# High parts of the weight pieces one step ahead of the low parts, and a down ring turned by two banks

## The chip, the cores and the metric

The kernel runs on one core of a Trainium2 chip. The metric is the device time of one execution in microseconds (us). Three timed runs of the kernel before gave 2814.41 us as their median, with 2812.03 and 2814.73 us as the lowest and the highest. One more execution was recorded by the profiler; its own time was 2820.96 us and its span, from the first to the last recorded instruction, 2819.2 us.

## The reference

The program is one pre-norm transformer block in float32 on 2048 rows of width 576: softmax attention with 32 heads of 18 columns, then a gated feed-forward layer with 4608 hidden columns.

```python
h  = x + attention(layernorm(x), wqkv, wo)            # 32 heads, full softmax
n  = layernorm(h)                                     # no scale, no offset
g, u = n @ w_gate, n @ w_up                           # 576 -> 4608, both
h2 = h + (gelu(g) * u) @ w_down                       # 4608 -> 576
```

Only the feed-forward layer is touched by the change. It fills about the last 1200 us of the span.

## The kernel before, in words

**Numbers in two parts.** TensorE multiplies float16. To keep float32 precision every operand is scaled by a power of two and split: a high part (the value rounded to float16) and a low part (what the rounding left). A product is then the sum of high by high, low by high and high by low. For weights, ScalarE (ACT) writes the high part with one activation, and VectorE (DVE) writes the low part with one `scalar_tensor_tensor`, which reads the weight and the high part. The power of two comes from the largest magnitude of the piece: two DVE reductions, a transpose on TensorE (PE), and six to fifteen tiny DVE operations ("the tail").

**Chunks and units.** The 4608 hidden columns are cut into 18 chunks of 256, and two chunks make a pair. The rows are taken in two halves (0 and 1). `unit(c, p)` computes gate and up products of chunk c for one half, by a Strassen scheme: seven block products for gate, seven for up, each of seven 512-column matmuls. It has 14 steps, called m1 to m14 here, and each ends with a `yield`. It uses six PSUM banks: `g[0..2]` = `singles[0..2]` and `u[0..2]` = `more[0..2]`. After the products, ACT applies gelu, DVE multiplies by the up product ("gate", line 907), ACT writes the high part of the result (line 910) and POOL the low part (line 913). The last of these in a unit belong to `ag` and `au`: the DVE adds of lines 965 and 970, the gelu of line 904, the gate of line 907.

`down(p, dsc, last)` then multiplies the results of two chunks by two chunks of `w_down`: 16 products of twelve 288-column matmuls, each product into the next bank of `down_ring`, and each followed by one DVE operation (line 989) that adds it to the rows in `nat` and so frees the bank. A bank is taken again after four products. The twelve matmuls of one product take, for f = 0 to 3 in turn, (high result, `dh[f]`), (high result, `dl[f]`), (low result, `dh[f]`); `dh` and `dl` are the high and low part of `w_down`.

**The order of the work.** PE, ACT, DVE, POOL and the queue of SP run the instructions in the order in which the program emits them (`manual_schedule`). The preparation of the next weights is a chain of generators called `side`; `beside(main, side)` emits one step of the main generator and then one step of `side`. So a side step decides behind which main instructions its own instructions stand on each engine.

- `split_matrix(c, m)` prepares gate (m = 0) or up (m = 1) of chunk c: five steps of `exponents` (a reduction in the first; a reduction in the second; the transpose in the fifth), a "ready" step with the tail, and three steps that each write the high and low part of some of the seven pieces (lines 826 to 837). In the first of these (k = 0) `then()` starts the load of the next matrix into the same buffer `W8`; for the last matrix it stands at k = 2 and loads `w_down` (line 854).
- `split_down` prepares `w_down`: five steps of `exponents`, one with the tail (lines 862 to 872), four that write `dh[f]` and `dl[f]`, and at the end `blank_rows()`, a small memset on POOL.

One pair runs as `unit(c, 1)` beside the first six steps of the next gate matrix; then `unit(c+1, 1)`, `down(1)`, `unit(c+2, 0)` and `unit(c+3, 0)` beside one chain (line 1117); then `down(0)` beside nothing. The chain has 13 slots in `unit(c+1, 1)` (none after m14), 14 in `down(1)` (none after its first two products), and 14 in each of the two units: 55. It needs

```python
g2 3, pause 2, u2 9, pause 2, g3 9, pause 2, u3 9, pause 5, dn 10     # sum 51
```

slots, where g2, u2 are gate and up of chunk c+2, g3, u3 of chunk c+3, and dn is `split_down`. What is left of the chain when the last unit ends is emitted at once (`run(dn)`), ahead of `down(0)`. The same generators, with the same pauses of five, prepare the first chunks in a longer chain (line 1079) that ends with `rows1()`, which makes the rows of half 1.

Of the kernel before, what the change touches and what calls it, by code (L numbers as in the profile page):

```python
# [14 lines left out]
AF = mybir.ActivationFunctionType  # L15
# [16 lines left out]
def tile_block(  # L32
# [18 lines left out]
    nc = tc.nc  # L51
# [22 lines left out]
    singles = [ps.tile([P, 512], F32, name=f"bank{i}") for i in range(4)]  # L74
# [4 lines left out]
    def ring(items):  # L79
        while True:  # L80
            yield from items
# [12 lines left out]
    def view(region, off, shape, dtype=None):  # L94

        dtype = dtype or region.dtype
        v = region if dtype == region.dtype else region.bitcast(dtype)
        size = 4 if dtype == F32 else 2
        n = math.prod(shape)
        assert off % size == 0  # L100
        v = v[:, off // size : off // size + n]
        if len(shape) == 2:
            v = v.rearrange("p (a b) -> p a b", b=shape[1])
        elif len(shape) == 3:
            v = v.rearrange("p (a b c) -> p a b c", b=shape[1], c=shape[2])
        return v
# [11 lines left out]
    def exponents(views, name, space=2):  # L118

        after = 1 if space == 2 else 0  # L120
        n = len(views)
        k = views[0].shape[1]
        ac = small.tile([P, n, k], F32, tag=f"ac{n}_{k}", name=f"ac_{name}")
        am = small.tile([P, n], F32, tag=f"am{n}", name=f"am_{name}")
        for i, v in enumerate(views):
            for c in range(k):
                nc.vector.tensor_reduce(ac[:, i, c : c + 1], v[:, c], axis=AX.X, op=ALU.max,
                                        apply_absolute_value=True)
                if i + 1 < n or c + 1 < k:
                    yield  # L130
        nc.vector.tensor_reduce(am, ac, axis=AX.X, op=ALU.max)
        for _ in range(2 * space - after):
            yield
        pt = next(m_ring)
        for i in range(n):
            nc.tensor.transpose(pt[:, i * P : (i + 1) * P], am[:, i : i + 1].to_broadcast([P, P]), id32)
        for _ in range(after):
            yield
        ab = small.tile([P, n], F32, tag=f"ab{n}", name=f"ab_{name}")
        nc.vector.tensor_reduce(ab, pt[:, : n * P].rearrange("o (n p) -> o n p", n=n),  # L140
                                axis=AX.X, op=ALU.max)
        nc.vector.tensor_scalar_max(ab, ab, 2.0 ** -60)
        e = small.tile([P, n], I32, tag=f"e_{name}", name=f"e_{name}")
        nc.vector.tensor_scalar(e, ab.bitcast(I32), 23, None, op0=ALU.logical_shift_right)
        return e
# [139 lines left out]
    def result(it):  # L285
        while True:
            try:
                next(it)
            except StopIteration as end:
                return end.value  # L290
# [114 lines left out]
    with tc.manual_schedule(engines={EngineType.SP}):  # L405
        n0, n1, n2 = norm_w(0), norm_w(1), norm_w(2)
        s = [None, None]
# [27 lines left out]
        s = [None, result(n1)]  # L435
# [335 lines left out]
    df = view(A, W8O, (4, D))  # L771
# [7 lines left out]
    dh = view(W, 6 * 2 * S, (4, D), F16)  # L779
    dl = view(W, 6 * 2 * S + 2 * 4 * D, (4, D), F16)  # L780
# [3 lines left out]
    def blank_rows():  # L784
        nc.gpsimd.memset(W8[3 * KR :, 4:, 2], 0.0)
# [14 lines left out]
    def split_matrix(c, m, hi_on=None, then=None, at=0, space=2):  # L800

        wh, wl = slots[c % 2][m]
        sums = [(nc.gpsimd.tensor_add, S1, A21, A22), (nc.gpsimd.tensor_sub, S2, S1, A11),
                (nc.gpsimd.tensor_sub, S3, A11, A21), (nc.gpsimd.tensor_sub, S4, A12, S2)]

        def add():
            if sums:
                op, d, a, b = sums.pop(0)
                op(W8[:, d], W8[:, a], W8[:, b])  # L809

        it = exponents([view(A, W8O + 4 * 4 * KT * P, (2, 2 * KT * P))], f"m{m}", space)
        while True:
            add()
            try:
                next(it)
            except StopIteration as end:
                e = end.value
                break
            yield
        while sums:  # L820
            add()
        nc.vector.tensor_copy(ee[:, m, c % 2 : c % 2 + 1], e)
        s = pow2(e, -1, 266, f"s_m{m}")
        yield "ready"
        r = slice(2 * KR, 3 * KR)
        for k, (a, b) in enumerate(((4, 7), (0, 2), (2, 4))):
            if hi_on is None:
                nc.scalar.activation(wh[:, a:b], W8[:, a:b], AF.Copy, scale=s)  # L828
            else:
                hi_on(wh[:, a:b], W8[:, a:b], s)  # L830
            nc.vector.scalar_tensor_tensor(wl[:, a:b], W8[:, a:b, :2], s, wh[:, a:b, :2],  # L831
                                           op0=ALU.mult, op1=ALU.subtract)
            nc.vector.scalar_tensor_tensor(wh[r, a:b, 2], W8[r, a:b, 2], s[r], wh[r, a:b, 2],  # L833
                                           op0=ALU.mult, op1=ALU.subtract)
            if k == at and then is not None:
                then()
            yield
        if m == 0:
            scales[c % 2] = (pow2(e, 1, -20, f"gsc{c % 2}"), pow2(e, -1, 228, f"hsc{c % 2}"))
# [9 lines left out]
    def pause(n):  # L849
        for _ in range(n):  # L850
            yield
# [7 lines left out]
    def split_down(sc):  # L859

        ed = yield from exponents([view(A, W8O + 4 * 2 * D * i, (1, 2 * D)) for i in range(2)], "dn")
        E = small.tile([P, 2], I32, tag="E", name="E")
        nc.vector.tensor_add(E, ee[:, 0], ee[:, 1])
        nc.vector.tensor_add(ed, ed, E)
        M = small.tile([P, 1], I32, tag="M", name="M")
        nc.vector.tensor_max(M, ed[:, 0:1], ed[:, 1:2])
        nc.vector.tensor_sub(E, E, M.to_broadcast([P, 2]))
        nc.vector.tensor_scalar(E, E, 1, 268, op0=ALU.mult, op1=ALU.add)
        nc.vector.tensor_scalar_max(E, E, 0)
        s = pow2(E, 1, 0, "s_dn")  # L870
        dscs.append(pow2(M, 1, -262, "dsc"))
        yield
        for f in range(4):
            sf = s[:, f // 2 : f // 2 + 1]
            nc.scalar.activation(dh[:, f], df[:, f], AF.Copy, scale=sf)
            nc.vector.scalar_tensor_tensor(dl[:, f], df[:, f], sf, dh[:, f],
                                           op0=ALU.mult, op1=ALU.subtract)
            yield
        blank_rows()
# [133 lines left out]
    side = iter(())  # L1013
# [6 lines left out]
    for n in range(NS):  # L1020
# [3 lines left out]
        for kt in range(NT):  # L1024
# [28 lines left out]
            if n == 2 and kt == 4:  # L1053
                side = prepare_wo()
# [3 lines left out]
            if n == NS - 2 and kt == NT // 2:  # L1058
                by = nc.vector.tensor_scalar_mul
                side = chain(split_matrix(0, 0, by, lambda: load_matrix(w_up, 0, nc.gpsimd), space=6), pause(10),  # L1060
                             split_matrix(0, 1, by, lambda: load_matrix(w_gate, 1, nc.gpsimd), space=6),
                             pause(10), until_ready(second))
# [11 lines left out]
    more = [ps2.tile([P, 512], F32, name=f"more{i}") for i in range(4)]  # L1074
    banks += singles[:3] + more[:3]
    m_ring = ring([singles[3], more[3]])
    down_ring = ring([singles[1], more[1], singles[0], more[0]])
    it = unit(0, 0)
    side = chain(second, pause(5), split_matrix(1, 1, None, lambda: load_down(0, nc.gpsimd), 2),
                 pause(5), split_down(0), rows1())  # L1080
# [22 lines left out]
    for sc in range(NCH // 2):  # L1103
        c = 2 * sc
        last = sc == NCH // 2 - 1
        dsc = dscs[-1]
        if not last:
            g2, g3 = (split_matrix(c + 2, 0, None, lambda c=c: load_matrix(w_up, c + 2)),
                      split_matrix(c + 3, 0, None, lambda c=c: load_matrix(w_up, c + 3)))
            u2, u3 = (split_matrix(c + 2, 1, None, lambda c=c: load_matrix(w_gate, c + 3)),  # L1110
                      split_matrix(c + 3, 1, None, lambda sc=sc: load_down(sc + 1), 2))
            dn = split_down(sc + 1)
            side = chain(until_ready(g2))
        beside(unit(c, 1), side)
        run(side)
        if not last:
            side = chain(g2, pause(2), u2, pause(2), g3, pause(2), u3, pause(5), dn)
        beside(islice(u := unit(c + 1, 1), 13), side)
        run(u)
        beside(down(1, dsc, last), side, head=2)  # L1120
        if last:
            break
        run(u2)
        beside(unit(c + 2, 0), side)
        run(u3)
        beside(unit(c + 3, 0), side)
        run(dn)
        if sc + 2 < NCH // 2:
            load_matrix(w_gate, c + 4)
        beside(down(0, dscs[-1], sc == NCH // 2 - 2), iter(()))  # L1130
# [26 lines left out]
```

## Time and profile before

| what | value |
|---|---|
| median of three runs | 2814.41 us (2812.03 to 2814.73) |
| profiled execution: time, span | 2820.96 us, 2819.2 us |
| granted TensorE clock, mean over the span | 0.987 |
| PE busy, share of the span | 94% |
| DVE, ACT, POOL busy | 78%, 54%, 24% |
| PE busy in 200 us of the feed-forward part | 196.5 to 196.9 us |
| distance of one pair from the next | 134.8 us |

A row of the timeline gives the start and length of an instruction (or of a run of equal ones), its engine, its line, what it writes and reads, and in brackets the idle time of the engine before it with the engine, tile and line that ended the wait. A row of the waits gives the total, the number and the longest. "PEclk" is the TensorE clock granted, as a share of full speed. [...]

### The profile page before, as it was taken

Reading aid. Unit: us, or ns where it says so; the run is one execution under the profiler, and the core shown is the slowest. Engines: PE = TensorE matmul, PEld = TensorE weight load, DVE = VectorE, ACT = ScalarE, POOL = GpSimd, SP = SyncE. Lnnn points to the kernel's source line nnn. Section 1 sums busy time; section 2 is a strip of 40 time slices with the busy share of each in tenths; the row PEclk is TensorE's granted clock in tenths of the full one; section 3 lists DMA queues with packets and bytes.
Section 4 is the critical chain, followed back from the end, with each engine's and each line's share of the span. In section 5 each row is a group of like instructions: output and inputs, shape, how many; then the busy total and the mean of one; then the engine's idle time right before and its main releaser. Section 6 shows DMA issues by size and latency. Waiting matters only on the chain.

```text
span 2819.2 us, 43701 instructions
## 1 busy us (share of the span) xinstructions
PE 2645.4 (94%) x16665; PEld 1094.8 (39%) x16665; DVE 2188.8 (78%) x3950; ACT 1515.8 (54%) x1872; POOL 682.9 (24%) x833
## 2 busy tenths in 40 slices
PE   6899999999999999999997789999999999999999
PEld 3542222222222222222233345555555555555555
DVE  6369999999999999999978657575757575656563
ACT  5216877777777777777754324333334333333332
POOL 2101432211222122211215333232322222322211
PEclk9999999999999999999999899999999999999999
DMA  8211110100101010000014131010101010101011
GB/s 220 75 50 41 39 39 14 29 19 15 39 12 36 14 39 14 25 22 18 25 30 110 53 76 48 11 48 21 39 21 40 22 46 21 38 22 38 21 57 39
DMA packets 162823, 111.99 MB, mean 40 GB/s; under 512 B 82612, under 2 KB 141620, under 8 KB 162612
## 3 DMA queue, kind: packets, MB, share of 16 engines
q1 hardware_dynamic: 150479, 95.30, 12.3%
q0 software_dynamic: 7296, 12.66, 1.7%
q8 instruction: 130, 2.13, 0.3%
q10 hardware_dynamic: 4837, 1.25, 0.2%
q14 instruction: 81, 0.66, 0.1%
HBM read 74.45 MB, written 14.42 MB: 32 GB/s over the span
## 4 chain that ended last, share of the span: by engine, by line
DVE 51%; PE 42%; DMA 3%; ACT 2%; issue 1%; SPq 1%; POOL 0%; ACTq 0%; DVEq 0%; POOLq 0%
DVE mx L535 42%; PE bank L899 12%; PE more L899 12%; PE bank L279 8%; PE more L279 5%; PE pair L279 4%; DVE W L833 1%; ACT W L828 1%; DMA X<-A 1%; PE bank L532 1%; DVE W L831 1%; DVE nat L989 1%; PE bank L585 1%; DVE st L186 1%; DVE WK L831 1%
## 5 line engine op out<-in xcount | busy, mean ns | idle before, releaser
L535 DVE TENSOR_REDUCE mx<-bank 128x1 f32<-128x512 f32 x2048 | 1264.9, 682 | 29.1 <-PE bank L532 29.1
L581 ACT ACTIVATE WK<-pair 128x1024 f32<-128x1024 f32 x1024 | 991.5, 1021 | 303.4 <-PE pair L579 303.1
L585 PE MATMUL bank<-WK,V 128*32 128x512 f32 x4096 | 548.3, 607 | 0.2 <-ACT nat L599 0.2
L279 PEld LDWEIGHTS <-WK 128*128 128x128 f16 x3456 | 338.7, 98 | 109.0 <-issue 16.3
L899 PEld LDWEIGHTS <-W 128*128 128x128 f16 x2394 | 235.0, 98 | 283.5 <-issue 8.2
L532 PE MATMUL bank<-W 54*128 54x512 f16 x1024 | 291.5, 382 | 40.0 <-DVE mx L535 10.0
L532 PE MATMUL bank<-A 54*128 54x512 f16 x1024 | 280.4, 382 | 37.2 <-DVE mx L535 6.3
L585 PEld LDWEIGHTS bank<-WK,V 128*32 128x32 f32 x4096 | 81.0, 108 | 437.9 <-issue 411.4
L279 PE MATMUL bank<-W,WK 128*128 128x288 f16 x1728 | 236.7, 287 | 14.2 <-DVE nat L989 10.8
L279 PE MATMUL more<-W,WK 128*128 128x288 f16 x1728 | 235.5, 286 | 3.4 <-DVE nat L989 3.4
L608 POOL TENSOR_TENSOR rp<-rc,minus_one 128x16 f32<-128x16 f32 x28 | 81.8, 2923 | 612.3 <-DMA rc<-nat 612.3
L899 PE MATMUL more<-X,W 128*128 128x512 f16 x792 | 223.8, 379 | 0.0
L899 PE MATMUL more<-V,W 128*128 128x512 f16 x720 | 203.2, 380 | 0.0
L809 POOL TENSOR_TENSOR A<-A 128x384 f32<-128x384 f32 x144 | 143.3, 1016 | 172.2 <-ACT V L920 100.4
L913 POOL TENSOR_TENSOR WK<-tmp,WK 128x512 f16<-128x512 f32 x73 | 88.0, 1206 | 332.3 <-ACT WK L910 325.2
L579 PE MATMUL pair<-W 56*128 56x512 f16 x1024 | 157.2, 379 | 3.6 <-ACT WK L581 2.8
L532 PEld LDWEIGHTS <-W 54*128 54x128 f16 x1024 | 59.7, 93 | 247.9 <-issue 219.6
L579 PE MATMUL pair<-A 56*128 56x512 f16 x1024 | 154.2, 376 | 0.2
L917 ACT COPY tmp<-bank 128x512 f32<-128x512 f32 x36 | 20.9, 582 | 237.5 <-PE bank L899 237.5
L532 PEld LDWEIGHTS <-A 54*128 54x128 f16 x1024 | 57.2, 93 | 235.1 <-issue 205.9
L828 ACT ACTIVATE W<-A,p_s_m 128x768 f16<-128x768 f32 (+1 forms) x78 | 78.2, 1036 | 105.6 <-DVE p_s_m L171 105.6
L989 DVE SCALAR_TENSOR_TENSOR nat<-more,p_dsc,nat 128x288 f32<-128x288 f32 x144 | 74.2, 515 | 77.7 <-PE more L279 77.1
(261 smaller groups left out, 2892.6 us busy)
## 6 DMA issues: line engine op xcount, KB each, us to landing
A<-in_B_w_down_dram SPq DMA_DIRECT2D x8, 1152.0 KB
nat<-rc SPq DMA_DIRECT2D x32, 256.0 KB
A<-in_B_w_gate_dram SPq DMA_DIRECT2D x64, 128.0 KB
A<-in_B_w_up_dram SPq DMA_DIRECT2D x64, 128.0 KB
qk_hi<-qk SPq DMA_DIRECT2D x36, 128.0 KB
qk_lo<-qk SPq DMA_DIRECT2D x36, 128.0 KB
out_dram<-nat SPq DMA_DIRECT2D x16, 288.0 KB
X<-nat SPq DMA_DIRECT2D x100, 36.0 KB
```

The source lines that it names most:

```text
L279: nc.tensor.matmul(dst, a, b, start=(i == 0), stop=(i == len(pairs) - 1))
L532: nc.tensor.matmul(pms[j][:, :TB], Q[r, q0 : q0 + P], K[r, kc * TB : (kc + 1) * TB], start=True, stop=True)
L535: nc.vector.tensor_reduce(mx[:, t, 2 * pr + j, kc : kc + 1], pms[j][:, :TB], axis=AX.X, op=ALU.max)
L579: nc.tensor.matmul(pS[:, j, :TB], K[r, kt * P : (kt + 1) * P], Q[r, qc * TB : (qc + 1) * TB], start=True, stop=True)
L581: nc.scalar.activation(pes[(2 * kt + pr) % NPE], pS[:, :, :TB], AF.Exp, scale=ex_reg)
L585: nc.tensor.matmul(acc[32 * hh : 32 * hh + 32, :TB], Vg[n // NB][:, kt * G4 + hh * VC : kt * G4 + hh * VC + 32], pes[(2 * kt + hh // 2) % ...
L608: nc.gpsimd.tensor_tensor(rc, den, minus_one.to_broadcast([P, R]), op=ALU.pow)
L809: op(W8[:, d], W8[:, a], W8[:, b])
L828: nc.scalar.activation(wh[:, a:b], W8[:, a:b], AF.Copy, scale=s)
L899: nc.tensor.matmul(bank, w, x_, start=start and i == 0, stop=i == len(mm) - 1, skip_group_check=not start)
L913: nc.gpsimd.tensor_sub(hl[:, 2 * i + j], v, hh[:, 2 * i + j])
L989: nc.vector.scalar_tensor_tensor(nat[:, t, ws], pt[:, :HALF], dsc, nat[:, t, ws], op0=ALU.mult, op1=ALU.add)
```

## The change

For weights whose high part ACT writes, the high part of the first piece is now emitted in a step of its own, and each later step emits the high part of the next piece together with the low part of the present one. So `split_matrix` has four such steps where it had three, and `split_down` five where it had four. `then()` stays behind the low part of its k, one step later than before. Weights whose high part DVE itself writes (the first two matrices, `hi_on` given) keep their order.

`down_ring` starts with `singles[0], more[0]` in place of `singles[1], more[1]`, so that of the 16 products the last two go to `singles[1]` and `more[1]` rather than to `singles[0]` and `more[0]`. The pause ahead of dn is four steps where it was five (line 1117 only). The chain of a pair now needs

```python
g2 4, pause 2, u2 10, pause 2, g3 10, pause 2, u3 10, pause 4, dn 11  # sum 55
```

```diff
@@ split_matrix
-        for k, (a, b) in enumerate(((4, 7), (0, 2), (2, 4))):
+
+        def high(a, b):
             if hi_on is None:
                 nc.scalar.activation(wh[:, a:b], W8[:, a:b], AF.Copy, scale=s)
             else:
                 hi_on(wh[:, a:b], W8[:, a:b], s)
+
+        cuts = ((4, 7), (0, 2), (2, 4))
+        if hi_on is None:
+            high(*cuts[0])
+            yield
+        for k, (a, b) in enumerate(cuts):
+            if hi_on is not None:
+                high(a, b)
+            elif k + 1 < len(cuts):
+                high(*cuts[k + 1])
             nc.vector.scalar_tensor_tensor(wl[:, a:b], W8[:, a:b, :2], s, wh[:, a:b, :2],
                                            op0=ALU.mult, op1=ALU.subtract)
@@ split_down
         yield
+        sf = [s[:, f // 2 : f // 2 + 1] for f in range(4)]
+        nc.scalar.activation(dh[:, 0], df[:, 0], AF.Copy, scale=sf[0])
+        yield
         for f in range(4):
-            sf = s[:, f // 2 : f // 2 + 1]
-            nc.scalar.activation(dh[:, f], df[:, f], AF.Copy, scale=sf)
-            nc.vector.scalar_tensor_tensor(dl[:, f], df[:, f], sf, dh[:, f],
+            if f < 3:
+                nc.scalar.activation(dh[:, f + 1], df[:, f + 1], AF.Copy, scale=sf[f + 1])
+            nc.vector.scalar_tensor_tensor(dl[:, f], df[:, f], sf[f], dh[:, f],
                                            op0=ALU.mult, op1=ALU.subtract)
             yield
         blank_rows()
@@ the rings and the chain
-    down_ring = ring([singles[1], more[1], singles[0], more[0]])
+    down_ring = ring([singles[0], more[0], singles[1], more[1]])
-            side = chain(g2, pause(2), u2, pause(2), g3, pause(2), u3, pause(5), dn)
+            side = chain(g2, pause(2), u2, pause(2), g3, pause(2), u3, pause(4), dn)
```

## Prediction

> **What bounds the kernel now.** The first line of the page gives the span; a windows answer over one pair then gives busy time by stage (columns: stretch, its length, then busy us and count of PE, PEld, DVE, ACT and POOL, PEclk, DMA).
>
> ```profile
> span 2819.2 us, 43701 instructions
> 2008.53:2051.15 42.62, 42.62 (x199) 19.58 (x199) 29.93 (x58) 21.86 (x34) 12.41 (x12) 1.00 0.13 41
> 2051.15:2074.67 23.52, 23.52 (x193) 18.79 (x192) 9.13 (x17) 0.76 (x2) 5.08 (x6) 1.00 0.07 21
> 2074.67:2117.20 42.53, 42.53 (x201) 19.48 (x199) 24.17 (x47) 19.56 (x30) 11.21 (x11) 1.00 0.06 18
> 2117.20:2143.43 26.23, 23.95 (x195) 18.91 (x194) 20.02 (x40) 5.91 (x7) 6.32 (x6) 1.00 0.16 46
> ```
>
> The stages are two units of half 0, `down(0)`, two units of half 1, `down(1)`. PE sets the pace and has no gap in the first three; only `down(1)` loses time, 26.23 - 23.95 = 2.28 us in a pair of 134.9. More than about 8 x 2.3 = 18 us isn't there to be won in the repeated part. The waits from 1500 us on (total, number, longest) name them.
>
> ```profile
> PE bank L279 <- DVE nat L989: 10.8, 9, 2.6
> PE bank L899 <- DVE pi_gsc L169: 9.6, 8, 1.2
> ```
>
> The timelines around the first show a relay between ACT and DVE:
>
> ```profile
> 2116.30 1.02 DVE L831 SCALAR_TENSOR_TENSOR WK<-A,p_s_m,W 128x768 f16<-128x768 f32 x1 [0.65 <-ACT W L828]
> 2117.35 1.39 DVE L833 SCALAR_TENSOR_TENSOR W<-A,p_s_m,W 32x384 f16<-32x384 f32 x1
> 2118.77 0.69 DVE L965 TENSOR_TENSOR WK<-bank,WK 128x512 f32<-128x512 f32 x1
> 2119.50 0.72 ACT L904 ACTIVATE WK<-WK,p_gsc 128x512 f32<-128x512 f32 x1 [2.72 <-DVE WK L965]
> 2120.13 0.92 ACT L828 ACTIVATE W<-A,p_s_m 128x768 f16<-128x768 f32 x1
> 2121.08 0.75 DVE L831 SCALAR_TENSOR_TENSOR WK<-A,p_s_m,W 128x512 f16<-128x512 f32 x1 [1.62 <-ACT W L828]
> 2123.75 0.51 DVE L989 SCALAR_TENSOR_TENSOR nat<-bank,p_dsc,nat 128x288 f32<-128x288 f32 x1
> 2124.31 1.63 PE L279 MATMUL bank<-W,WK 128*128 128x288 f16 x12 [1.07 <-DVE nat L989]
> ```
>
> The low part of u2 (k = 0) holds up the add at 2118.77; the gelu waits for that add, the next high part stands behind the gelu, the next low part behind that. The first down product began at 2117.20, yet its rows are added at 2123.75, and the fifth product waits for that bank.
>
> **Step 1, the ring.** At the end of `down(1)`, the 13th and the 15th product are added here:
>
> ```profile
> 2139.45 0.52 DVE L989 SCALAR_TENSOR_TENSOR nat<-bank,p_dsc,nat 128x288 f32<-128x288 f32 x1
> 2142.85 0.52 DVE L989 SCALAR_TENSOR_TENSOR nat<-bank,p_dsc,nat 128x288 f32<-128x288 f32 x1
> 2143.43 0.81 PE L899 MATMUL bank<-X,A 128*128 128x512 f16 x3 [1.20 <-DVE pi_gsc L169]
> ```
>
> The next unit starts in `singles[0]`. That is the bank of product 15 now (free at 2143.37, PE at 2143.43) and of product 13 in the changed order (free at 2139.97, before PE gets there). The scale the wait is put down to isn't read by a matmul; it only stands behind that add. Products 15 and 16 go to `g[1]`, `u[1]`, which m3 and m4 need 3 us later. At the other end `down` begins in `g[0]`, `u[0]`, last read by the gelu of m11 and the gate of m12, both over by then. So the ring takes the whole 9.6 us.
>
> **Step 2, the first wait.** u2 now has its high part in slot 13 (after m13) and its low parts in slots 14 to 16, behind down products 3 to 5. DVE goes from m12's gate to the tail, the add of m13, the add and gate of m14, and is ready for the first row add when product 1 is; the three low parts (1.02 + 0.61, then twice 0.75 + 0.48) lie between row adds of 0.51 that come every 1.47 us, and each bank is free over 2 us before it is taken again. Of the 10.8 us one 2.6 belongs to the first pair; 8.2 us go.
>
> **Step 3, what is late next.** The four matrices take four steps more, the pause gives one back: dn starts in slot 45 where it started in 42, its tail moves from 47 to 50, its last low part from 51 to 55, which is behind m14 of the last unit, directly ahead of `down(0)`. Until now 8 us of matmuls covered it. DVE rows of that unit before (tail from L140 to L171):
>
> ```profile
> 2029.78 1.67 PE L899 MATMUL bank<-X,W 128*128 128x512 f16 x7
> 2037.76 0.42 DVE L140 TENSOR_REDUCE ab_dn<-bank 128x2 f32<-128x256 f32 x1
> 2038.77 1.16 POOL L913 TENSOR_TENSOR WK<-tmp,WK 128x512 f16<-128x512 f32 x1 [5.36 <-ACT WK L910]
> 2038.88 1.07 DVE L866 TENSOR_TENSOR M<-e_dn 128x1 int32<-128x1 int32 x1
> 2041.04 0.15 DVE L171 TENSOR_SCALAR p_dsc<-pi_dsc 128x1 int32<-128x1 int32 x1
> 2044.42 0.69 DVE L946 TENSOR_TENSOR A<-bank,A 128x512 f32<-128x512 f32 x1 [1.08 <-ACT A L945]
> 2045.09 0.82 DVE L876 SCALAR_TENSOR_TENSOR W<-A,p_s_dn,W 128x576 f16<-128x576 f32 x1
> 2046.72 0.75 DVE L907 SCALAR_TENSOR_TENSOR A<-tmp,p_hsc,A 128x512 f32<-128x512 f32 x1
> 2051.15 1.63 PE L279 MATMUL bank<-W,WK 128*128 128x288 f16 x12
> ```
>
> The tail lasted 3.43 us, 0.9 of them L866 until POOL's row ended, so 2.5 alone. It now stands behind m9's add (2044.42, fixed by PE and ACT) and everything after it queues on DVE in this order: add 0.69, tail 2.5, add 0.69, gate 0.75, low 0.82, gate 0.75, low 0.82, add 0.69, low 0.82, add 0.69, gate 0.75, low 0.82: 10.8 us. From one start to the next the rows lose or gain under 0.1 us (2044.42 to 2045.09 is 0.67), so I leave the sum: the last `dl` is ready at 2055.2. No high part is later: the last follows the gelu (0.72) on the third add. The first down product reaches the matmul that reads `dl[3]`, its eleventh, at 2051.15 + 10 x 0.1225 (1.47 a product) = 2052.4. PE stands 2.8 us, and all of `down(0)` behind that matmul; DVE's row adds wait with it and lose nothing more. With 0.08 us saved at each of the eleven seams it is 2.0. POOL's three subtractions of 1.16 now run beside low parts and the last gate, as it ran beside L833 at 2117.35 (1.39 where its equal at other places takes 0.61). That row lost 0.78; 1.2 us in all is my upper bound for it, so 4.0. I take 3.2 us, nearer the plain sum: eight pairs, +25.6 us (+16 to +32).
>
> [...]
>
> **Step 4, loads and queues.** SP's load of `w_down` sits behind the low parts of u3, in slot 40 instead of 36 (6.0 us later), on a DVE about 1 us behind:
>
> ```profile
> 2025.18 0.37 SPq L854 DMA_DIRECT2D A<-in_B_w_down_dram  x1
> A<-in_B_w_down_dram POOLq DMA_DIRECT2D x1, 1152.0 KB, 6.1
> ```
>
> 2032.2 + 6.1 = 2038.3; two reductions (2.7) and 0.2 end at 2041.2, the transpose is due after m8, at 2041.9: hidden by 0.7 us, and each further us would stop PE. SP has nothing behind it until the next gate load, which waits for the last low part (2055.2 for 2048.2) and has all of `down(0)`. `blank_rows` on POOL moves behind m14, where nothing waits for it. The gate and up loads move by one to three steps and keep 2 us or more ahead of their transposes: nothing.
>
> **Step 5, the first chunks.** Their chain gets three steps more and no pause back, and low parts now fall behind the row statistics:
>
> ```profile
> 1593.49 0.79 POOL L854 DMA_DIRECT2D A<-in_B_w_down_dram  x1 [23.13 <-DVE st L186]
> 1603.11 0.43 PE L136 MATMUL more<-id,am_dn 128*128 128x128 f32 x2 [1.13 <-DVE am_dn L131]
> 1676.04 0.32 PE L136 MATMUL bank<-id,am_m 128*128 128x128 f32 x1 [2.90 <-DVE am_m L131]
> ```
>
> That load starts some 5 us later, its transpose two unit steps (3 us) later, so PE waits about 2 us more there; the rows of half 1 start later, but a copy that stood behind their transposes goes ahead. Between -2 and +5 us; I take +1.5.
>
> **Sum.** -9.6 - 8.2 + 25.6 + 1.5 = +9.3 us, on the profiled 2820.96: 2830.3. The median is 6.55 below the profiled run: 2823.7 us, say 2824.
>
> **Rivals.** *The cover is enough (other side).* If dn's tail ran two unit steps (3.0 us) earlier, in the DVE idle time before 2044.42, `dl[3]` would land in time and the gains stay: 2814.4 - 17.8 + 1.5 = 2798. It decides from a wait of 0.7 us down; for it speaks DVE's 12.7 us of idle in 42.6; against it that program order keeps the tail behind m9's add. *A wash.* At a wait of 2.2 us loss and gain cancel: 2815. For it: 2.0 is within the bounds. *The clock drops too.* After a longer stop PE ran slow:
>
> ```profile
> 1656.00:1665.00 9.00, 5.62 (x45) 4.36 (x45) 5.84 (x16) 1.00 (x2) 0.00 (x0) 1.00 0.50 97
> 1672.00:1676.00 4.00, 1.13 (x6) 0.29 (x3) 2.08 (x4) 0.00 (x0) 1.05 (x2) 1.00 0.19 54
> 1676.00:1680.00 4.00, 3.96 (x13) 1.66 (x14) 3.13 (x9) 2.30 (x4) 4.00 (x4) 0.66 0.00 0
> ```
>
> A stop of 2.90 us (row 1676.04) was followed by a granted clock of 0.66 over 4 us, 1.4 us lost; stops summing to 3.4 us in nine were not. Eight such: +11, 2835. For it: 3.2 is longer than 2.90; against: a few matmuls fall into the stop. [...] *The ring doesn't help:* if the 1.2 us is some other wait, 2833; the row adds speak against it.
>
> **How the numbers follow.** Under 0.2%, 5.6 us, a change can't be told from none. Chances: forecast (2818 to 2831) 0.50, wash 0.22, clock 0.11, cover 0.13, ring 0.04. Slower 0.62 (some of the forecast's lower edge is within 0.2%), same 0.25, faster 0.13. The likeliest case alone is 2816 to 2831; the range, with the lowest sum of the bounds (2820.96 - 17.8 + 16 - 2 less 6.55, 2811) and most of the clock's, is 2808 to 2836.
>
> **What would show it.** Right: no wait for `pi_gsc` at a unit's first product, none at the fifth of `down(1)`, DVE's waits for line 828 nearly gone, a new wait of about 3 us in each `down(0)`'s first product for `dl`'s line, pairs near 135.8 us. A `down(0)` that starts without a wait makes the prediction wrong; a wait at the transpose of dn would show Step 4 wrong.

## The result and the profile after

The changed kernel takes 2841.85 us (median of four runs, 2837.11 to 2844.21) beside 2814.47 us for the kernel before: a ratio of 1.0097 with a 95% interval of 1.0080 to 1.0115. It is slower by some 27 us; 9.3 us had been forecast, and the time lies above the stated range. In a later comparison on one chip the ratio was 1.0081 (1.0067 to 1.0095). The median of the kernel before differed from one comparison to the next (2814.5, 2819.7, 2819.7, 2821.9 us), so below each kernel is held against the kernel before that ran beside it.

The profiled executions took 2820.96 us before and 2844.21 us after: 23.25 us more. First the page's span, then the stages of one pair of chunks in the order of before: two units of half 0, `down(0)`, two units of half 1, `down(1)` (columns as before).

```profile
span 2842.4 us, 43702 instructions
2014.72:2057.34 42.62, 42.62 (x202) 19.50 (x199) 29.31 (x61) 20.00 (x33) 11.48 (x10) 1.00 0.14 45
2057.34:2085.29 27.95, 25.06 (x190) 19.21 (x189) 12.04 (x21) 2.35 (x4) 6.73 (x7) 0.94 0.09 27
2085.29:2127.83 42.54, 42.54 (x202) 19.58 (x201) 23.74 (x47) 18.53 (x29) 11.98 (x11) 1.00 0.06 18
2127.83:2151.35 23.52, 23.52 (x192) 18.68 (x191) 15.78 (x34) 6.26 (x8) 5.38 (x6) 1.00 0.11 32
```

`down(1)` has lost its gaps. `down(0)`, which had none, has taken 27.95 us in this row where it took 23.52, and its PE is idle for 2.89 us. Its clock column reads 0.94, and in spite of the idle time its busy time has grown too, from 23.52 to 25.06. The waits of PE from 1500 us on name the new one; the two rows of before (`nat L989` at the fifth product, `pi_gsc`) have no successor in the repeated part, from 1750 us on:

```profile
PE bank L279 <- DVE W L890: 23.1, 16, 1.7
```

Line 890 writes `dl`. Sixteen waits are two in each of eight pairs. Here is one on PE:

```profile
2057.34 1.02 PE L279 MATMUL bank<-W,WK 128*128 128x288 f16 x7
2059.59 0.53 PE L279 MATMUL bank<-W,WK 128*128 128x288 f16 x3 [1.23 <-DVE W L890]
2061.78 0.41 PE L279 MATMUL bank<-W,WK 128*128 128x288 f16 x2 [1.66 <-DVE W L890]
2062.02 2.71 PE L279 MATMUL more<-W,WK 128*128 128x288 f16 x12
2064.52 2.27 PE L279 MATMUL bank<-W,WK 128*128 128x288 f16 x12
```

The first product stops at its eighth matmul for `dl[2]` and at its eleventh for `dl[3]`; the two stops together are called the stop below. Then the second product takes 2064.52 - 2062.02 = 2.50 us from start to start, where one at a clock of 1.00 takes 1.47 (and is recorded with 1.63, so that neighbours overlap): the clock has dropped. Six microseconds from the end of each of the eight stops on, three of the eight rows (the eight read 0.77, 0.51, 0.72, 0.72, 0.77, 0.51, 0.72, 0.72 for PEclk):

```profile
1786.57:1792.57 6.00, 6.00 (x39) 4.33 (x39) 1.55 (x3) 0.00 (x0) 1.61 (x2) 0.77 0.38 110
1923.41:1929.41 6.00, 6.00 (x26) 3.72 (x26) 1.03 (x2) 0.00 (x0) 1.62 (x2) 0.51 0.39 113
2061.78:2067.78 6.00, 6.00 (x36) 4.25 (x36) 1.55 (x3) 0.00 (x0) 1.61 (x2) 0.72 0.40 115
```

What the clock lacks of 1.00 in the eight rows adds up to 2.56, times 6 us: 15.4 us. PE is busy for all of the 6.00 us in each of these rows; its matmuls don't wait, they only run slowly; in steps of 0.2 us the clock column reads 0.50 for 3.4 or 6.8 us at each stop and 1.00 around that.

The change did what it was made for: from 1750 us on, VectorE's waits for the high parts that ACT writes in `split_matrix` sum to 53.8 us before (line 828) and to 16.3 after (the same line is 829 there); the seven waits that are left were there before. These waits were not what set the time.

### The profile page after: what moved, and what is told of

It reads as the page before. It is cut to its first block, busy times and chain, and to the rows that moved or that the text cites. A ratio compares the mean times of both kernels' runs of the same rounds, so it can differ in the third digit from the quotient of the medians.

```text
span 2842.4 us, 43702 instructions
## 1 busy us (share of the span) xinstructions
PE 2666.9 (94%) x16665; PEld 1102.3 (39%) x16665; DVE 2170.4 (76%) x3950; ACT 1512.9 (53%) x1872; POOL 686.7 (24%) x833
## 5 line engine op out<-in xcount | busy, mean ns | idle before, releaser
L279 PEld LDWEIGHTS <-WK 128*128 128x128 f16 x3456 | 345.4, 100 | 138.9 <-issue 27.7
L279 PE MATMUL bank<-W,WK 128*128 128x288 f16 x1728 | 246.2, 292 | 31.6 <-DVE W L890 23.1
L279 PE MATMUL more<-W,WK 128*128 128x288 f16 x1728 | 245.8, 294 | 4.1 <-DVE nat L1003 4.0
L1003 DVE SCALAR_TENSOR_TENSOR nat<-bank,p_dsc,nat 128x288 f32<-128x288 f32 x144 | 74.4, 517 | 98.0 <-PE bank L279 97.1
```

The costliest lines, as they stand in the source:

```text
L279: nc.tensor.matmul(dst, a, b, start=(i == 0), stop=(i == len(pairs) - 1))
L1003: nc.vector.scalar_tensor_tensor(nat[:, t, ws], pt[:, :HALF], dsc, nat[:, t, ws], op0=ALU.mult, op1=ALU.add)
```

## The experiments

Two questions were open: what each part of the change is worth, and whether the time beyond the stop is the clock. Where a line number differs from the kernel before, the statement is the same and its line has moved.

### The ring alone (e1)

```diff
 # the kernel before
-    down_ring = ring([singles[1], more[1], singles[0], more[0]])
+    down_ring = ring([singles[0], more[0], singles[1], more[1]])
```

> The kernel before with only the ring turned. Theory (the 1.2 us at the start of a pair is a wait for the bank of the 15th down product): it goes in all eight pairs, 2814.5 - 9.6 = 2805 us, and the fifth product of down(1) still waits 1.07 us. Rival (the wait is for something else): 2814.5 us, the 1.2 us stay.

Measured: 2809.08 us beside 2819.70, ratio 0.9961 (0.9950 to 0.9972): 10.6 us less. The waits of PE from 1500 us on keep the one at the fifth product and have no row for `pi_gsc` any more:

```profile
PE bank L279 <- DVE nat L989: 10.8, 9, 2.5
```

So the wait that the profile put down to the scale was one for the 15th product's bank, as the prediction had it.

### The order alone (e2)

```diff
 # the changed kernel
-    down_ring = ring([singles[0], more[0], singles[1], more[1]])
+    down_ring = ring([singles[1], more[1], singles[0], more[0]])
```

> The changed kernel with the ring as before. Prediction as made (each part is worth its own term): the 1.2 us come back, 2841.9 + 9.6 = 2851 us. Rival (the new order alone puts the 15th product's row add ahead of the low parts of g3, so the bank is free in time without the ring): 2842 us within 3, no wait at the start of a pair.

Measured: 2843.38 us, ratio 1.0086 (1.0068 to 1.0104), with no wait at the start of a pair; the changed kernel's later ratio is 1.0081. The rival expectation held. DVE and PE at the end of a `down(1)`:

```profile
2147.52 0.52 DVE L1003 SCALAR_TENSOR_TENSOR nat<-bank,p_dsc,nat 128x288 f32<-128x288 f32 x1 [0.95 <-PE bank L279]
2147.95 1.01 DVE L842 SCALAR_TENSOR_TENSOR W<-A,p_s_m,W 128x768 f16<-128x768 f32 x1
...
2148.79 1.67 PE L913 MATMUL bank<-X,A 128*128 128x512 f16 x7
```

The 15th product's row add (2147.52) now stands ahead of g3's first low part (2147.95), so its bank is free before the next unit begins at 2148.79. The ring and the new order remove the same wait; beside the new order the ring adds nothing.

This run holds one more answer. It has the stop of the changed kernel, 2.18 or 2.19 us from one restart of PE to the next in each of the eight pairs. Seven times the six microseconds behind it read 0.50 to 0.77 for PEclk. The first time they do not:

```profile
1784.93:1790.93 6.00, 6.00 (x49) 4.79 (x49) 2.07 (x4) 0.00 (x0) 1.63 (x2) 1.00 0.37 109
```

The stop is there and the clock holds; what that pair took stands in the table of the pairs below.

### PE kept busy during the stop (e4)

Twelve matmuls into a bank that nobody reads fill the two stops; the stop itself can't shrink.

```diff
 # the changed kernel, first product of each down(0)
-                    run(accumulate(pt[:, :HALF], pairs))
+                        for q, (a, b) in enumerate(pairs):
+                            for _ in range({7: 5, 10: 7}.get(q, 0)):
+                                nc.tensor.matmul(singles[3][:, :512], id16, XT[:, 0, :512], start=True, stop=True)
+                            nc.tensor.matmul(pt[:, :HALF], a, b, start=q == 0, stop=q == 11)
```

> The changed kernel with twelve more matmuls of 512 columns, into a bank that nobody reads, in the two stops of each first product of down(0): five ahead of its 8th matmul, seven ahead of its 11th. They add 2.6 us of PE work to 2.9 us of stop, so the stop itself stays. Clock theory (the stop is followed by some 3.4 us or more at half clock, 2.0 us lost in a pair): granted clock near 1.0 after the stop, 8 x 2.0 = 16 us less, 2826 us. Rival (the time beyond the stop comes from elsewhere): 2842 us or a little more.

Measured: 2828.61 us, ratio 1.0029 (1.0017 to 1.0042), 14.8 us below e2, which has the same stops and ran beside it. The stop and the six microseconds after it:

```profile
2052.97:2057.41 4.44, 4.14 (x23) 2.15 (x22) 4.29 (x6) 2.36 (x4) 1.21 (x2) 1.00 0.01 4
2057.41:2063.41 6.00, 6.00 (x49) 4.79 (x49) 2.07 (x4) 0.00 (x0) 1.63 (x2) 1.00 0.38 106
```

The first down product still takes its 4.4 us, but the granted clock is 1.00 throughout, here and in the six microseconds behind each of the other seven stops. The time beyond the stop is the clock's.

### Cover on PE's side (e5)

```diff
 # the changed kernel, down(0)
+        if spread:
+            open_ = [(i, n, next(down_ring)) for i in range(2) for n in range(2)]
+            for i, n, pt in open_:
+                for q, (a, b) in enumerate(down_pairs(0, i, n)[:6]):
+                    nc.tensor.matmul(pt[:, :HALF], a, b, start=q == 0, stop=False)
+            for i, n, pt in open_:
+                for q, (a, b) in enumerate(down_pairs(0, i, n)[6:]):
+                    nc.tensor.matmul(pt[:, :HALF], a, b, start=False, stop=q == 5)
...
```

> The changed kernel, but the first four products of down(0) take their matmuls for f = 0 and 1 in four banks first (2.9 us of work) and those for f = 2 and 3 after that, so that the late low part has cover on PE. Theory: the stop of 2.9 us and the half clock behind it both go, 2841.9 - 23 - 16 = 2803 us. Rival (the wait only moves to a later product, or the half clock has another cause): 2825 to 2842 us.

Measured: 2811.24 us, ratio 0.9968 (0.9956 to 0.9979), 8.5 us below the kernel before. In the repeated part one short wait is left in each pair:

```profile
PE bank L1006 <- DVE W L890: 6.8, 8, 0.8
```

With 2.9 us of matmuls put in front, 23.1 us of recorded waits become 6.8, and the clock reads 1.00 behind all eight of them. The forecast of 2803 us was too low by this rest.

### dn three steps earlier, and the first chain as before (e3, e6, e8)

```diff
 # e3, and e8
-            side = chain(g2, pause(2), u2, pause(2), g3, pause(2), u3, pause(4), dn)
+            side = chain(g2, pause(1), u2, pause(1), g3, pause(1), u3, pause(4), dn)
 # e6, and e8: the first chain with high and low part in one step
-        if hi_on is None:
+        if hi_on is None and ahead:
             high(*cuts[0])
             yield
...
+    # second, split_matrix(1, 1, ...) and split_down(0) are called with ahead=False
```

> The changed kernel with the three pauses of two steps between the matrices cut to one, so that dn and all its parts come three steps (4.5 us of matmuls) earlier and the loads come earlier with them. Theory: the last low part lands in time, no stop in down(0), no half clock there: the changed kernel's time less 23 - 16, that is 15 to 18 us below the kernel before, plus 1 to 5 us for the first chain. Rival (the low parts of u2 fall back between the unit's last adds and the first wait of down(1) returns): 8 us more than that.

> The changed kernel, but the chain of the first chunks (up of chunk 1 and the first w_down, and gate of chunk 1) keeps high and low part in one step as before. Theory (the first chain got three steps longer, its w_down load and its rows of half 1 start later): 2 to 5 us less than the changed kernel. Rival (other waits of that stretch hide it): within 1 us of the changed kernel.

> Both: pauses of one between the matrices, and the first chain as before. Theory: all gains of the change and none of its costs, 15 to 18 us below the kernel before. Rival: a wait at a transpose or in down(1) takes back 8 us or more.

Measured, beside 2819.70 us: e3 2803.73 (0.9938, 0.9922 to 0.9955), e6 2840.15 (1.0066, 1.0049 to 1.0083), e8 2801.90 (0.9931, 0.9915 to 0.9948). With dn back under its cover neither e3 nor e8 has a wait in the repeated part but a single one of 1.0 us. What the first chain costs was measured once more, with the changed kernel beside it:

> The changed kernel itself, beside its variants on one chip: 1.0097 of the kernel before within 0.002, as in its first runs.

> The changed kernel with the first chain as before, beside the changed kernel: 2 to 5 us less if the longer first chain costs what Step 5 said at its upper half; under 1 us less if other waits hide it.

> The changed kernel with pauses of one between the matrices and the first chain as before, beside the others: 17 to 18 us below the kernel before.

Beside 2821.92 us: the changed kernel 2843.51 (1.0081, as expected), the same with the old first chain 2840.20 (1.0074, 1.0061 to 1.0088), with both edits 2802.59 (0.9928, 0.9914 to 0.9941). The first chain's share is 3.3 us by these medians and 1.8 by e3 and e8. The intervals of the ratios overlap in both comparisons, so it isn't shown that the longer first chain costs anything; if it does, it is a few microseconds.

### Only the pause cut (e9)

```diff
 # the changed kernel
-... u3, pause(4), dn)
+... u3, pause(1), dn)
```

> The changed kernel with the pause ahead of dn cut from four steps to one: dn comes three steps earlier, but the load of w_down does not. Theory (the load is issued 2.4 us into the last unit, takes 6.1 us, and two reductions follow, so the transpose after m5 isn't fed before 11.4 us while PE is there at 7.6): the stop in down(0) goes, and PE waits 3 to 4 us at dn's transpose instead, in all eight pairs, with a half clock after it as well: within 10 us of the changed kernel. Rival (the load has room): the same time as with the pauses of one.

Measured: 2843.86 us, ratio 1.0079 (1.0063 to 1.0096). The stop in `down(0)` is gone; PE waits for dn's reductions instead. Waits of PE from 1750 us on, then one of them and the 6 us after it:

```profile
PE bank L136 <- DVE am_dn L131: 12.3, 4, 3.3
PE more L136 <- DVE am_dn L131: 11.4, 4, 3.0
```

```profile
2044.65:2047.68 3.03, 0.00 (x1) 0.00 (x1) 2.82 (x4) 0.00 (x0) 0.00 (x0) 0.88 0.00 0
2047.68:2053.68 6.00, 6.00 (x15) 2.33 (x16) 4.91 (x16) 3.16 (x6) 1.16 (x1) 0.50 0.00 0
```

Eight waits of 3.0 us, each with a lower clock behind it (0.50 to 0.73 in the eight rows of 6 us), cost what the stop had cost. dn can't be moved alone; its load has to come with it, as in e3.

### Only the place (e10)

```diff
 # the kernel before, with the turned ring
-            side = chain(g2, pause(2), u2, pause(2), g3, pause(2), u3, pause(5), dn)
+            side = chain(g2, pause(3), u2, pause(2), g3, pause(2), u3, pause(4), dn)
```

> The kernel before with the ring turned and the pause ahead of u2 three steps instead of two (the one ahead of dn four instead of five): u2's first high and low part, still in one step, stand behind m13 and the others behind the third and fourth down product; dn keeps its place and has its full cover. Theory (where the low parts stand is what counts): the fifth product of down(1) no longer waits, 17 us below the kernel before, level with the changed kernel with shorter pauses. Rival (the separation of high and low is what counts): the wait of 1 us stays and only the ring's 10 us are gained.

Measured: 2798.92 us (2795.81 to 2802.93), ratio 0.9923 (0.9909 to 0.9936). That is 23.0 us below the kernel before, where 17 had been expected. From 1750 us on PE waits for nothing that the profile lists. This is the fastest kernel of the study, level with e8 and e8b within the intervals, though high and low part still stand in one step. DVE and PE around the end of the unit:

```profile
2106.22 0.68 DVE L965 TENSOR_TENSOR WK<-bank,WK 128x512 f32<-128x512 f32 x1
2108.83 1.02 DVE L831 SCALAR_TENSOR_TENSOR WK<-A,p_s_m,W 128x768 f16<-128x768 f32 x1 [1.94 <-ACT W L828]
2111.92 0.51 DVE L989 SCALAR_TENSOR_TENSOR nat<-bank,p_dsc,nat 128x288 f32<-128x288 f32 x1
...
2113.17 1.63 PE L279 MATMUL bank<-W,WK 128*128 128x288 f16 x12
```

The low part still waits 1.94 us for ACT. But the add of m13 (2106.22) now runs ahead of it, the gelu with it, and the first row add ends at 2112.43, before the fifth product wants the bank at 2113.17. From 1750 us on, the waits of VectorE for line 828 still sum to 46.9 us, and PE doesn't notice. The wait of VectorE for ScalarE, which the separation removes, costs nothing by itself here.

### The pairs side by side

The transpose of dn comes once in a pair, so two of them in a row give a pair's length. For the changed kernel, e4 and e10:

```profile
2048.05 0.38 PE L136 MATMUL bank<-id,am_dn 128*128 128x128 f32 x2
2185.24 0.38 PE L136 MATMUL more<-id,am_dn 128*128 128x128 f32 x2
```

```profile
2043.69 0.38 PE L136 MATMUL bank<-id,am_dn 128*128 128x128 f32 x2
2179.20 0.38 PE L136 MATMUL more<-id,am_dn 128*128 128x128 f32 x2
```

```profile
2027.43 0.38 PE L136 MATMUL bank<-id,am_dn 128*128 128x128 f32 x2
2159.74 0.38 PE L136 MATMUL more<-id,am_dn 128*128 128x128 f32 x2
```

| kernel | length of a pair, us (lowest to highest of seven) | what it has |
|---|---|---|
| e10 | 132.30 to 132.31 | no wait |
| e1 | 133.4 to 133.7 | the wait at the fifth product |
| e5 | 133.3 | a rest of the stop |
| before | 134.6 to 135.0, mean 134.84 | both waits |
| e4 | 135.51 to 135.52 | the stop, full clock |
| e2, its first pair alone | 135.51 | the stop, full clock |
| after | 136.8 to 138.4, mean 137.42 | the stop and the half clock |

The first pair of e2, where the clock held without any added matmul, took what the pairs of e4 took; so the twelve matmuls of e4 change nothing but the clock. In the changed kernel, what the clock row behind a stop lacks of 1.00, times 6 us, also gives the length of that pair beyond 135.5 us to within 0.1 us: 1.38 for 1.33 us at 0.77, 2.94 for 2.85 at 0.51, 1.68 for 1.64 to 1.68 at 0.72.

From the table the change in a pair is: both waits gone, 134.84 - 132.30 = 2.54 us; the stop, 135.51 - 132.30 = 3.21 us; the clock, 137.42 - 135.51 = 1.91 us. Over eight pairs these are -20.3, +25.7 and +15.3, together +21. With 1.8 to 3.3 us for the first chain, if it costs that, this is 22 to 24 us, and the two profiled executions differ by 23.25.

## Why the prediction was right and wrong

**The sign and the stop were right.** Step 3 said that the last low part of `w_down` would stand behind m14 and that the eleventh matmul of the first down product would wait for it. It does, in all eight pairs (the eighth waits too, for the low part before it; that delay lies within the same stop). The size was right as well, 3.2 us taken and 3.2 us measured. DVE and POOL of the changed kernel, from m9's add to the last low part:

```profile
2050.60 0.69 DVE L960 TENSOR_TENSOR A<-bank,A 128x512 f32<-128x512 f32 x1 [4.04 <-ACT A L959]
2051.21 0.41 DVE L140 TENSOR_REDUCE ab_dn<-bank 128x2 f32<-128x256 f32 x1
2052.32 0.16 DVE L877 TENSOR_TENSOR M<-e_dn 128x1 int32<-128x1 int32 x1
2053.58 0.15 DVE L171 TENSOR_SCALAR p_dsc<-pi_dsc 128x1 int32<-128x1 int32 x1
2055.91 1.16 POOL L927 TENSOR_TENSOR WK<-A,WK 128x512 f16<-128x512 f32 x1 [9.79 <-ACT WK L924]
2056.55 1.14 DVE L890 SCALAR_TENSOR_TENSOR W<-A,p_s_dn,W 128x576 f16<-128x576 f32 x1
2057.77 1.15 POOL L927 TENSOR_TENSOR WK<-tmp,WK 128x512 f16<-128x512 f32 x1 [0.69 <-ACT WK L924]
2058.21 1.32 DVE L890 SCALAR_TENSOR_TENSOR W<-A,p_s_dn,W 128x576 f16<-128x576 f32 x1
2060.91 0.81 DVE L890 SCALAR_TENSOR_TENSOR W<-A,p_s_dn,W 128x576 f16<-128x576 f32 x1
```

The tail shrinks to 2.5 us (2051.21 to 2053.73), because its tensor-tensor step takes 0.16 instead of 1.07 once POOL is idle. From the add to the end of the last low part it is 11.1 us, 10.8 by the sum. Two low parts stretch to 1.14 and 1.32 beside POOL where one alone takes 0.81: 0.84 us together is what the trace shows. The bound of 1.2 us in Step 3 was the author's estimate; no run shows it. The seams gave back some 0.5 us. Step 3 had bounded these two and not computed them, so that 3.2 came out to a tenth is in part luck. The two stretched low parts end 0.62 and 0.61 us after the POOL rows that they overlap (2057.07 and 2058.92), less than the 0.81 of one alone; what stretches them is not shown.

**Step 1 was right alone and wrong as a term of its own.** The ring takes the whole wait, as e1 shows, but the order takes it as well (e2). The sum is not hurt, since the wait was counted once; the prediction's view that the two parts of the change have a term each was wrong.

**Step 2 was right in effect.** The wait at the fifth product goes, and it goes because u2's low part moves behind the add of m13. Step 2 described that place, but not that the place alone is enough: separating high from low is not needed for it (e10). Both gains were sized a little too small, 17.8 us in the sum and 20.3 by the pairs. A recorded wait begins when the recorded matmul ends, and a down product is recorded with 1.63 us where it takes 1.47 from start to start, so each of the sixteen waits leaves out about 0.16 us.

**Step 4 held.** No wait at dn's transpose in the repeated part, and e9 shows how little room there was: with dn 4.5 us earlier and the load where it was, PE waits 3.0 us, so some 1.5 us were to spare where the working had 0.7.

**Step 5 isn't contradicted**: 1.8 and 3.3 us by the medians lie within its bounds, but the runs don't set them apart from nothing.

**The step that failed is the sum: it prices each stop at its own length and has nothing for the clock.** The drop of the clock stood beside it as a rival with a chance of 0.11 and 11 us. It was no rival but part of the case: in the changed kernel the clock fell at every one of the eight stops, and that cost 15 us. On the profiled executions the forecast was 2830.3 us and 2844.21 were measured, 13.9 more; the clock's 15 less the 2.5 by which the gains were larger make up most of it.

Two sentences misled. "A few matmuls fall into the stop" was held against the drop; the runs show that three matmuls, 0.53 us recorded, in the 3.4 us from 2058.36 to 2061.78 did not keep the clock up, nor did they in the other seven stops, while twelve more do (e4). And stops summing to 3.4 us in a row of nine, which had left the clock at 1.00, were taken as a counterexample; but in that row 5.6 us of matmuls ran, and neither of its two stops was longer than 2.6 us. The price was low too: 1.4 us read from a row of 4 us, where the low clock takes 1.4 to 2.9 us, 1.9 on average. With the clock's 15 us added, the forecast's own terms give -17.8 + 25.6 + 1.5 + 15 = +24 us.

## What to carry to other kernels

Moving a piece of preparation later by a few steps is paid where its cover ends: count the steps to the last consumer before counting what the move saves, and move the load that feeds it too. When a stop of PE of about 3 us is forecast, count the slower matmuls behind it as well as the stop; in this case they took 1.91 us in a pair beside the stop's 3.21, three fifths more. A wait of one helper engine for another, here VectorE for ScalarE, is worth removing only if the engine that sets the pace stands at its end; here the turned ring and one step of pause at the right place gained 0.8% and left that wait in place.

## What the runs showed of the hardware that was not expected

The granted clock fell in or just behind stretches in which PE was not wholly idle: 0.53 us of matmuls in 3.4 us were not enough to hold it, in the eight stops of the changed kernel and in seven of the eight of e2. The first stop of e2, as long as the others, left it at 1.00, so what falls into the stop does not decide it alone. In e9 eight stops of 3.0 us were followed by 0.50 to 0.73.

It stood at 0.50 for 3.4 us at six of the eight stops of the changed kernel and for 6.8 us at the second and the sixth. The fall came between some 1.0 us before PE's second restart and 0.6 us after it, with the stops equal to 0.01 us. The first three (second restarts at 1786.57, 1923.41 and 2061.78):

```profile
1785.94:1789.32 3.38, 2.75 (x12) 1.77 (x12) 1.09 (x2) 0.49 (x1) 1.67 (x2) 0.50 0.26 74
1922.46:1929.24 6.78, 5.83 (x25) 3.60 (x25) 1.93 (x4) 0.62 (x1) 1.67 (x2) 0.50 0.34 98
2062.42:2065.80 3.38, 3.38 (x17) 2.15 (x15) 0.83 (x2) 0.00 (x0) 0.97 (x2) 0.50 0.41 115
```

So the mean of the six microseconds behind a stop differs, 0.77 to 0.51, and the eight values are the same four in the same order twice. The lengths of the pairs, 136.8 to 138.4 us, differ by this alone, as e4 with its 135.51 to 135.52 shows. What sets the moment of the fall, and why one stop of e2 cost no clock, no run shows.
